# Semaphores from GpSimd to VectorE at the port the two engines share

## The chip, the cores and the metric

The kernel runs on one core of a Trainium2 chip. Five engines of the core take part: TensorE (PE; its weight loads are listed apart as PEld), VectorE (DVE), ScalarE (ACT), GpSimd (POOL) and SyncE (SP), which issues the DMA transfers. The metric is the device time of one execution in microseconds, the median of a few runs.

## The reference

Three layers follow one another, all in float32, for 4 batches of 448 positions:

```python
# 1. causal attention, 12 heads of 64
attn = softmax(mask(q @ k.T / 8)); x = attn @ v          # heads side by side: 768 columns
# 2. gated feed-forward
h = relu(x @ w_in)                                        # 1024 columns
conv = sum(conv_w[k] * shifted(h, k - 1) for k in range(3))
x = (h * sigmoid(conv)) @ w_out
# 3. four experts, each a causal attention with one head of 64, the two best by x @ w_gate
for e in range(4):
    a = softmax(mask((x @ wq[e]) @ (x @ wk[e]).T / 8))
    out += weight_of(e) * (a @ (x @ wv[e]) @ wo[e])
```

## The kernel before

The weights of layer 2's second product and of layer 3's projections are folded into one matrix at the start (`fold`). Operands of the large products are split in a high and a low part, so that each product becomes three matmuls: high by high, low by high, high by low (`products`, L990). For each batch, `ffn_in` makes eight chunks of the gated hidden layer: a ReLU on ACT (L1008), the convolution (L1014 on ACT, two steps of L1019 on DVE), tanh on ACT (L1034), the gate (L1027 on DVE, or L1024 and L1025 on POOL), then the high part (`high`, L696 on ACT, L698 on DVE or L700 on POOL) and the low part (`low`, L704 on DVE or POOL). The last 64 columns of a chunk are copied apart (the tile `gx`, L700 when POOL does it). `project` multiplies the chunks by the folded weights. Attention (`scores`, `norms`, `weigh`) runs on PE (L760 scores, L807 transposes, L838 values), DVE (L737 mask and maximum, L789 division) and ACT (L741 exponential).

Nothing in the code fixes the order of all this by hand. A class `Plan` collects about 4450 steps with their dependencies, their estimated cost on each engine that may do them, and their buffers. `schedule` plays the steps forward in time: each engine takes the ready step of the highest rank. Some steps carry a port (`o.port`): every step that POOL may do counts as using the port when POOL does it, and DVE's steps of the classes copy, scale and subtraction out of SBUF and of the convolution count as using it on DVE. In the plan a step with the port starts only when the port's last user has ended, so that the planned times of such DVE steps and POOL steps do not overlap. `run` then emits all steps in order of planned start. What one engine issues is in that order; what holds between engines on the chip is only what the semaphores say. Besides those of the data there is one kind more: where a POOL step comes within 3 us of planned time behind a DVE step with the port, `run` makes POOL's first instruction wait by semaphore for DVE's last (`near`, `add_manual_dep`). In the other direction, DVE behind POOL, there was none.

Of the kernel before, what the change touches and what calls it, by code (L numbers as in the profile page):

```python
# [182 lines left out]
def noise(seed, n):  # L183

    x = (n * 2654435761 + seed * 40503 + 12345) & 0xFFFFFFFF
    for shift, factor in ((15, 0x2C1B3C6D), (12, 0x297A2D39), (15, 1)):
        x = ((x ^ x >> shift) * factor) & 0xFFFFFFFF
    return x / 2147483648.0 - 1.0
# [43 lines left out]
class Plan:  # L232
# [135 lines left out]
    def run(self):  # L368


        self.links()
        left = [(b, b.left) for t in self.tags.values() for b in t.made]
        kinds = {id(t.kind): (t.kind, dict(t.kind.free)) for t in self.tags.values()}

        def forward(rank):
            for b, n in left:
                b.left, b.ap = n, None
                for k in b.banks or ():
                    k.end, k.engine = 0.0, None
            for t in self.tags.values():  # L380
                t.next = t.live = 0
            for k, tiles in kinds.values():
                k.free = dict(tiles)
            return self.schedule(rank)

        rank = self.longest()
        length = forward(rank)
        best = (length, rank)
        for _ in range(ROUNDS):
            if length == float("inf"):  # L390
                break
            rank = self.backward()
            length = forward(rank)
            best = min(best, (length, rank))
        rank = list(best[1])
        forward(rank)
        begin = [o.start for o in self.ops]
        for seed, lo, hi, amp in SHIFTS:
            for o in self.ops:
                if seed < 0:  # L400
                    rank[o.n] += amp * (lo <= o.n < hi)
                elif lo <= begin[o.n] < hi:
                    rank[o.n] += amp * noise(seed, o.n)
        if SHIFTS and forward(rank) >= best[0]:
            forward(best[1])
        body, near = self.nc.cur_bb.bb, None
        for o in sorted(self.ops, key=lambda o: (o.start, o.n)):
            n = len(body.instructions)
            o.fn(o.engine)
            new = body.instructions[n:]  # L410
            if o.engine == "V" and "V" in o.port:
                near = o, new[-1].name
            elif o.engine == "G" and near and near[0].start > o.start - 3:
                self.tc.add_manual_dep(new[0], near[1], mybir.DependencyInfo(mybir.DependencyClass.Sync, mybir.DependencyReason.DATA), reason="port")

    def schedule(self, rank):
        for o in self.ops:
# [152 lines left out]
class Cost(dict):  # L570


    port = "V"
# [670 lines left out]
```

## Time and profile before

| | us |
|---|---|
| median of 3 runs | 521.71 (521.52 to 522.1) |
| the profiled execution | 521.82 |
| its span | 520.0 |
| PE busy | 510.4 (98%) |
| DVE busy | 416.7 (80%) |
| ACT busy | 357.4 (69%) |
| POOL busy | 79.3 (15%), 86 instructions |

The span is what the profiler saw of the program; the execution's own time is 1.8 us longer. Busy time is a sum over an engine's instructions and says nothing of what an instruction does in its time: one that is held counts as busy. PE's granted clock is at its upper level (2.4 GHz) throughout.

### The profile page before, as it was taken

How to read it: one execution, taken by the hardware profiler on the slowest of the kernel's cores; microseconds unless marked ns; L12 is line 12 of the kernel's file. 1: busy time of each engine (PE TensorE's matmuls, PEld its weight loads, DVE VectorE, ACT ScalarE, POOL GpSimd, SP SyncE). 2: the span in 40 equal slices, each digit the busy share in tenths (PEclk: the TensorE clock that was granted, in tenths of full speed). 3: DMA queues.
4: the chain of work that ended last, by engine and by line, in shares of the span. 5: the costliest groups of instructions: out<-in, count | busy, mean ns of one | idle time of the engine just before them, and what ended most of it. 6: DMA issues, size and time to landing. Idle time of an engine off the chain costs nothing.

```text
span 520.0 us, 10393 instructions
## 1 busy us (share of the span) xinstructions
PE 510.4 (98%) x3556; PEld 434.5 (84%) x3556; DVE 416.7 (80%) x1313; ACT 357.4 (69%) x1062; POOL 79.3 (15%) x86
## 2 busy tenths in 40 slices
PE   8799999999999999999999999999999999999997
PEld 4678888878888988999897878988888878999875
DVE  6999699999999098997478999996359999852681
ACT  2887377789999175863569988984269967532573
POOL 3122011242324000101014320130022001000000
PEclk9999999999999999999999999999999999999999
DMA  8885356674885100649101573663021505610052
GB/s 251 237 225 146 98 166 202 195 201 146 293 249 126 41 20 20 226 144 277 24 2 37 155 222 94 240 184 89 0 55 63 184 2 186 232 68 1 2 168 106
DMA packets 63524, 69.92 MB, mean 134 GB/s; under 512 B 36592, under 2 KB 57456, under 8 KB 63472
## 3 DMA queue, kind: packets, MB, share of 16 engines
q1 hardware_dynamic: 63472, 69.26, 44.6%
q8 instruction: 28, 0.46, 0.4%
q14 instruction: 24, 0.20, 0.1%
HBM read 55.87 MB, written 13.37 MB: 133 GB/s over the span
## 4 chain that ended last, share of the span: by engine, by line
PE 86%; DVE 8%; ACT 3%; DMA 1%; issue 1%; SPq 0%; ACTq 0%
PE pf L990 56%; PE bank L838 9%; PE bank L807 9%; PE bank L760 8%; DVE e L737 3%; PE pf L1187 2%; DVE e L789 2%; DMA work<-in_wqk 1%; ACT e L741 1%; PE pf L1098 1%; DVE z L698 1%; PE bank L990 1%; ACT e L786 1%; DVE pair L704 1%; PE pf L675 1%
## 5 line engine op out<-in xcount | busy, mean ns | idle before, releaser
L990 PE MATMUL pf<-pair,slab 128*128 128x448 f32 (+2 forms) x984 | 216.7, 366 | 0.9 <-ACT pair L696 0.7
L990 PEld LDWEIGHTS pf<-pair,slab 128*128 128x128 f32 x984 | 171.0, 188 | 18.6 <-ACT pair L696 1.2
L741 ACT ACTIVATE e<-e,stat 128x320 f32<-128x320 f32 (+3 forms) x256 | 127.1, 500 | 17.7 <-DVE stat L737 17.4
L737 DVE CUSTOM_DVE_ANT_0 e<-bank,mask 64x64 f32<-64x64 f32 (+3 forms) x256 | 93.1, 413 | 16.4 <-PE bank L760 15.6
L990 PE MATMUL pf<-pair,wqks 128*128 128x448 f32 x384 | 82.2, 370 | 0.0
L990 PEld LDWEIGHTS pf<-pair,wqks 128*128 128x128 f32 x384 | 70.9, 188 | 6.4 <-DVE pair L698 0.3
L807 PE MATMUL bank<-ident,e 128*128 128x128 f32 x448 | 71.0, 276 | 0.9 <-ACT e L741 0.2
L696 ACT ACTIVATE z<-bank 128x512 f32<-128x512 f32 (+1 forms) x133 | 53.2, 421 | 15.2 <-PE bank L838 8.5
L807 PEld LDWEIGHTS bank<-ident,e 128*128 128x128 f32 x448 | 53.7, 140 | 9.6 <-DVE stat L737 0.7
L704 POOL TENSOR_TENSOR pair<-work,pair 128x448 fp32r<-128x448 f32 (+1 forms) x35 | 42.6, 1236 | 87.4 <-DVE work L913 33.6
L786 ACT ACTIVATE e<-e,stat 64x64 f32<-64x64 f32 (+3 forms) x129 | 52.0, 448 | 4.6 <-DVE stat L781 3.6
L698 DVE COPY z<-bank 64x128 f32<-64x128 f32 (+1 forms) x91 | 38.0, 434 | 20.9 <-PE bank L807 11.9
L760 PE MATMUL bank<-pair,pair 64*128 64x448 f32 (+3 forms) x576 | 49.6, 291 | 0.0
L741 ACT ACTIVATION_READ_ACCUMULATOR e<-e,stat 128x1 f32 (+1 forms) x256 | 48.8, 191 | 0.0
L838 PE MATMUL bank<-z,block 128*64 128x448 f32 (+3 forms) x384 | 46.9, 386 | 0.0
L760 PEld LDWEIGHTS bank<-pair,pair 64*128 64x128 f32 (+1 forms) x576 | 42.4, 172 | 2.3 <-issue 0.8
L838 PEld LDWEIGHTS bank<-z,block 128*64 128x64 f32 x384 | 25.8, 136 | 21.0 <-issue 12.0
L1019 DVE SCALAR_TENSOR_TENSOR work<-hp,cws,work 128x448 f32<-128x448 f32 x64 | 42.8, 682 | 0.4
L990 PE MATMUL pf<-wvs,pair 128*128 128x260 f32 x288 | 39.6, 288 | 0.0
L700 POOL TENSOR_SCALAR pair<-work 128x896 fp32r<-128x896 f32 (+2 forms) x17 | 15.2, 895 | 145.4 <-DMA block<-in_vv 43.7
L990 PEld LDWEIGHTS pf<-wvs,pair 128*128 128x128 f32 x288 | 36.2, 189 | 0.5
L696 ACT ACTIVATE pair<-pf 64x448 fp32r<-64x448 f32 (+1 forms) x24 | 13.0, 542 | 32.0 <-PE pf L990 31.2
(98 smaller groups left out, 568.5 us busy)
## 6 DMA issues: line engine op xcount, KB each, us to landing
slab<-w_scratch SPq DMA_DIRECT2D x24, 768.0 KB, 4.6
work<-in_w_out SPq DMA_DIRECT2D x8, 768.0 KB, 4.9
work<-in_w_in SPq DMA_DIRECT2D x8, 768.0 KB, 6.0
w_scratch<-slab SPq DMA_DIRECT2D x8, 768.0 KB, 4.1
work<-in_qk SPq DMA_DIRECT2D x24, 224.0 KB, 4.4
work<-in_qk SPq DMA_DIRECT2D x48, 112.0 KB, 3.9
out<-work SPq DMA_DIRECT2D x23, 224.0 KB, 2.0
slab<-wo_scratch SPq DMA_DIRECT2D x6, 768.0 KB, 4.4
```

Source lines behind the costliest of these rows:

```text
L696: nc.scalar.activation(dst(), src(), AF.Copy)
L698: nc.vector.tensor_copy(dst(), src())
L700: nc.gpsimd.tensor_scalar(dst(), src(), 1.0, 1.0, op0=OP.mult, op1=OP.mult)
L704: return lambda e: engine(e).tensor_sub(dst(), src(), f32(h()))
L737: nc.vector.tensor_tensor_reduce(out=ec(o, c), in0=bank(o, c), in1=m, scale=-0.125, scalar=3.0e38, op0=OP.add, op1=OP.min, accum_out=st[ro ...
L741: nc.scalar.activation(ec(o, c), ec(o, c), AF.Exp, bias=st[rows, 0, o, c:c + 1], scale=-1.0, accum_out=st[rows, 1, o, c:c + 1])
L760: nc.tensor.matmul(bank(o, c), q(s)[own, Q0[c]:Q0[c] + QN[c]], k(t)[own, kc(o, c)], start=i == 0, stop=i == 2)
L786: nc.scalar.activation(dst(), src(), AF.Copy, scale=st[rows, 3, o, c:c + 1])
L807: P.op({"T": TURN}, lambda _: nc.tensor.transpose(dst(), src(), ident[:, :]), r=r, w=keys)
L838: nc.tensor.matmul(ps[own, S - n:S], v(k, o), z[:, 1024 * o + n0:1024 * o + n0 + n], start=k == 0, stop=k == 3)
L990: nc.tensor.matmul(out_ap(), a(), b(), start=first, stop=end), r=r, w=[(ps, 0)])
L1019: return lambda _: nc.vector.scalar_tensor_tensor(cv[:, :S], hp[:, i:S + i], cws[:, fc, i:i + 1], cv[:, :S], op0=OP.mult, op1=OP.add)
```

## The change

`near` becomes a record of the last step with the port on each of the two engines. A POOL step looks for the last DVE step with the port, as before; a DVE step with the port now looks for the last POOL step. If that one's planned start lies less than 3 us back, the new step's first instruction waits by semaphore for the other step's last. The order and the costs are not touched.

```diff
-        body, near = self.nc.cur_bb.bb, None
+        body, near = self.nc.cur_bb.bb, {}
...
-            if o.engine == "V" and "V" in o.port:
-                near = o, new[-1].name
-            elif o.engine == "G" and near and near[0].start > o.start - 3:
-                self.tc.add_manual_dep(new[0], near[1], mybir.DependencyInfo(mybir.DependencyClass.Sync, mybir.DependencyReason.DATA), reason="port")
+            if o.engine == "G" or o.engine == "V" and "V" in o.port:
+                other = near.get("VG"[o.engine == "V"])
+                if other and other[0].start > o.start - 3:
+                    self.tc.add_manual_dep(new[0], other[1], mybir.DependencyInfo(mybir.DependencyClass.Sync, mybir.DependencyReason.DATA), reason="port")
+                near[o.engine] = o, new[-1].name
```

No engine's instructions change their order; what changes are the semaphores that DVE's instructions wait for. A wait that another one implies is left out by the framework, so some rows also lose one. Line numbers after the change are one higher. Two places follow; a name in brackets is the engine whose semaphore a row waits for, and a number behind a tile's name is the buffer.

The first is DVE where the last chunks of batch 0's hidden layer are made, at about 161 to 163 us of the profile, before:

```order
L1027 SCALAR_TENSOR_TENSOR work_150<-work_150,hp_95 128x448 [waits Activation_49]
L698 CAST pair_134<-work_150 128x448 [waits DVE_49]
L704 TENSOR_TENSOR pair_134<-work_150,pair_134 128x448 [waits DVE_49]
L779 TENSOR_REDUCE stat_87<-stat_87 128x8 [waits Activation_49]
L781 RECIPROCAL stat_87<-stat_87 128x8 [waits DVE_49]
L789 TENSOR_SCALAR e_124<-e_124,stat_87 128x320 [waits DVE_49]
```

and after the change:

```order
L1028 SCALAR_TENSOR_TENSOR work_150<-work_150,hp_95 128x448 [waits Activation_49]
L699 CAST pair_134<-work_150 128x448 [waits Pool_49]
L705 TENSOR_TENSOR pair_134<-work_150,pair_134 128x448 [waits Pool_49]
L780 TENSOR_REDUCE stat_87<-stat_87 128x8 [waits Activation_49]
L782 RECIPROCAL stat_87<-stat_87 128x8 [waits DVE_49]
L790 TENSOR_SCALAR e_124<-e_124,stat_87 128x320 [waits DVE_49,Pool_49]
```

The cast (high part), the subtraction (low part) and the first division each wait for POOL now, each for another of the three `gx` copies, which POOL issues in a row and which waited for DVE already.

The second is DVE in the hidden layer of batch 2, at about 329 to 333 us, before:

```order
L698 COPY z_114<-bank_155 128x4x128 [waits PE_49]
L1019 SCALAR_TENSOR_TENSOR work_150<-hp_96,cws,work_150 128x448 [waits Activation_49]
L1027 SCALAR_TENSOR_TENSOR work_150<-work_150,hp_95 128x448 [waits Activation_49]
L1019 SCALAR_TENSOR_TENSOR work_150<-hp_96,cws,work_150 128x448 [waits DVE_49]
L779 TENSOR_REDUCE stat_87<-stat_87 128x8 [waits Activation_49]
L781 RECIPROCAL stat_87<-stat_87 128x8 [waits DVE_49]
L789 TENSOR_SCALAR e_124<-e_124,stat_87 128x320 [waits DVE_49]
```

and after the change:

```order
L699 COPY z_114<-bank_155 128x4x128 [waits PE_49]
L1020 SCALAR_TENSOR_TENSOR work_150<-hp_96,cws,work_150 128x448 [waits Activation_49,Pool_49]
L1028 SCALAR_TENSOR_TENSOR work_150<-work_150,hp_95 128x448 [waits Activation_49]
L1020 SCALAR_TENSOR_TENSOR work_150<-hp_96,cws,work_150 128x448 [waits DVE_49]
L780 TENSOR_REDUCE stat_87<-stat_87 128x8 [waits Activation_49]
L782 RECIPROCAL stat_87<-stat_87 128x8 [waits DVE_49]
L790 TENSOR_SCALAR e_124<-e_124,stat_87 128x320 [waits DVE_49,Pool_49]
```

One convolution step and one division got a wait for POOL, which at this time makes high parts of layer 1's operands for a later head pair and of this layer's chunks.

## Rows read from the trace of the kernel before

**Rows 1.** The page, part 1: busy time, share of the span, instructions.
```profile
PE 510.4 (98%) x3556; PEld 434.5 (84%) x3556; DVE 416.7 (80%) x1313; ACT 357.4 (69%) x1062; POOL 79.3 (15%) x86
```

**Rows 2.** Busy time by stretch: stretch, length, PE, PEld, DVE, ACT, POOL, clock, DMA, GB/s.
```profile
94.80:167.80 73.00, 72.87 (x503) 60.06 (x503) 72.05 (x214) 68.94 (x205) 24.94 (x25) 1.00 0.68 205
322.50:352.30 29.80, 29.80 (x172) 26.54 (x169) 29.43 (x89) 27.62 (x80) 5.74 (x7) 1.00 0.69 229
...
32.00:520.00 488.00, 483.78 (x3398) 417.06 (x3397) 390.40 (x1218) 337.17 (x1014) 69.97 (x73) 1.00 0.42 127
```

**Rows 3.** DVE's waits in 94.8:167.8, then 322.5:352.3: us in total, times, longest.
```profile
DVE e L737 <- PE bank L760: 0.3, 1, 0.3
...
DVE e L737 <- ACT work L1014: 0.5, 1, 0.5
```

**Rows 4.** Timeline of POOL and DVE near 98 and 129: start, us, what.
```profile
96.60 1.84 POOL L704 TENSOR_TENSOR slab<-work,slab 128x768 fp32r<-128x768 f32 x1
...
97.81 1.10 DVE L698 CAST pair<-work 128x896 fp32r<-128x896 f32 x1
...
127.84 1.85 POOL L704 TENSOR_TENSOR slab<-work,slab 128x768 fp32r<-128x768 f32 x1
...
129.39 0.79 DVE L1019 SCALAR_TENSOR_TENSOR work<-hp,cws,work 128x448 f32<-128x448 f32 x1
...
130.10 0.67 DVE L1019 SCALAR_TENSOR_TENSOR work<-hp,cws,work 128x448 f32<-128x448 f32 x1
```

**Rows 5.** Timeline of POOL and ACT near 438; in brackets the idle time before.
```profile
437.62 0.98 POOL L1025 TENSOR_TENSOR work<-work,hp 128x448 f32<-128x448 f32 x1
...
438.63 0.58 ACT L696 ACTIVATE pair<-work 128x448 fp32r<-128x448 f32 x1 [1.12 <-POOL work L1025]
```

**Rows 6.** Timeline of DVE and POOL near 162.
```profile
161.71 0.39 DVE L698 CAST pair<-work 128x448 fp32r<-128x448 f32 x1
...
161.77 0.49 POOL L700 TENSOR_SCALAR gx<-pair 128x128 fp32r<-128x128 f32 x1 [4.21 <-DVE work L1027]
...
162.14 0.62 DVE L704 TENSOR_TENSOR pair<-work,pair 128x448 fp32r<-128x448 f32 x1
...
162.26 0.66 POOL L700 TENSOR_SCALAR gx<-pair 128x128 fp32r<-128x128 f32 x1
...
162.90 0.30 POOL L700 TENSOR_SCALAR gx<-pair 128x128 fp32r<-128x128 f32 x1
```

**Rows 7.** Timeline of PE's weight loads (and one DVE cast); in brackets idle time before.
```profile
153.62 0.14 PEld L807 LDWEIGHTS bank<-ident,e 128*128 128x128 f32 x1 [0.21 <-DVE stat L737]
...
163.23 0.19 PEld L990 LDWEIGHTS pf<-pair,wqks 128*128 128x128 f32 x1
...
351.90 0.39 DVE L698 CAST pair<-work 128x448 fp32r<-128x448 f32 x1
...
352.35 0.19 PEld L990 LDWEIGHTS pf<-pair,wqks 128*128 128x128 f32 x1 [0.34 <-DVE pair L698]
```

**Rows 8.** Timeline of POOL and DVE in the second stretch.
```profile
329.43 0.94 POOL L700 TENSOR_SCALAR pair<-work 128x896 fp32r<-128x896 f32 x1 [17.75 <-DVE stat L737]
...
329.94 0.89 DVE L1019 SCALAR_TENSOR_TENSOR work<-hp,cws,work 128x448 f32<-128x448 f32 x1
...
349.41 0.96 POOL L700 TENSOR_SCALAR pair<-work 128x896 fp32r<-128x896 f32 x1 [1.78 <-DVE stat L779]
...
350.21 0.31 DVE L789 TENSOR_SCALAR e<-e,stat 128x192 f32<-128x192 f32 x1
```

**Rows 9.** Timeline of DVE and PE's weight loads near 239.
```profile
238.38 0.39 DVE L698 CAST pair<-work 128x448 fp32r<-128x448 f32 x1
...
239.86 0.19 PEld L990 LDWEIGHTS pf<-pair,wqks 128*128 128x128 f32 x1
```

**Rows 10.** Waits of PE's weight loads, 160 to 320: us in total, times, longest.
```profile
PEld bank L807 <- DVE stat L737: 0.5, 1, 0.5
PEld bank L807 <- ACT e L741: 0.4, 1, 0.4
```

## The prediction

> **What bounds the kernel now.** I read the busy times of the page first: TensorE (PE) is busy for 510.4 us of a span of 520.0, VectorE (DVE) for 416.7 [rows 1]. An average of 80% would say that DVE has room, so I looked at stretches. From 94.8 to 167.8 us DVE is busy for 72.05 of 73.00 us while PE is busy for 72.87, and from 322.5 to 352.3 for 29.43 of 29.80 [rows 2]. In each of them DVE waits for another engine once, for 0.3 and 0.5 us, both at its beginning [rows 3]. There DVE is a second bound: what is added to one of its instructions reaches all that follow, until DVE next waits for somebody. So the question is not how much DVE time is added in all, but how much in these stretches, and which PE instruction reads DVE's last result just in time.
>
> **What GpSimd and DVE do to each other before.** The change concerns places where the plan puts a GpSimd (POOL) step shortly ahead of a DVE step that needs the port. Two kinds of row show what happens there without a semaphore.
>
> In the first kind DVE comes second and is held inside its instruction. A subtraction on POOL starts at 127.84 and takes 1.85, so it ends at 129.69. DVE's L1019 starts at 129.39, takes 0.79 instead of the 0.67 that the same instruction takes right after it, and ends at 130.18, 0.49 after POOL's end [rows 4]. So it is held, but not for its whole length: about 0.18 of it is over when POOL ends. The copy at 97.81 is the same case: it ends at 98.91, 0.47 after POOL's 98.44 [rows 4].
>
> In the second kind DVE comes first, by a few hundredths, and POOL is held. At 161.71 DVE starts a cast (0.39), at 161.77 POOL starts a gx copy that takes 0.49; the next pair, 162.14 and 162.26, is alike, POOL taking 0.66. The third copy, at 162.90, meets no DVE instruction of this kind in its beginning and takes 0.30 [rows 6].
>
> **The change part by part.** No instruction is added, removed or moved on PE, ACT, SP or POOL; DVE's rows keep their order too, and 37 of them wait for POOL where 21 did. DVE waits in its order, so every DVE instruction behind such a wait stands with it. 34 POOL steps are now awaited by a first DVE step. I laid their ends beside the starts of those DVE instructions: for 14 POOL had ended before, and such a wait costs nothing. That leaves 20.
>
> *Price of a hand-off.* The trace has no tight wait of DVE for POOL. The nearest rows are ACT's wait for POOL, 437.62 + 0.98 = 438.60 to 438.63, so 0.03 [rows 5], and from below nothing (POOL long done); from above POOL's own wait for DVE: the cast ends at 162.10, POOL starts at 162.26, so 0.16 [rows 6]. I take 0.03, as the waiting engine is the one that reacts and POOL is the slow one to start. Then the first kind costs 0.03 + 0.67 - 0.49 = 0.21 for an L1019, and 0.15 to 0.25 for the other forms: DVE's instruction now begins after POOL has ended, where before it had begun and stood ready.
>
> The Trainium skill, page "SBUF — State Buffer", section "Who interferes with whom", says that the pair of ports is an exclusive lock, and that whichever comes second is blocked until the first is finished. By it the DVE instruction would have run its full length after POOL's end already, and a wait would add the hand-off alone. The rows agree that there is a lock and that POOL is held too, but not that the whole length comes after. What it would make of the time is the first rival below.
>
> *Stretch 1, until 153.6.* Overlaps of the first kind at 97.81, 129.39 and 142.78 (the first two in [rows 4], the third read alike) add 0.18 + 0.21 + 0.16 = 0.55 to DVE. At 153.62 PE's weight load waits for DVE (0.21 of idle time behind it) [rows 7]: no slack, so PE is 0.55 later.
>
> *Stretch 1, the three gx copies.* At 157.4 there is one more of the first kind, 0.21. Then the plan's order is DVE cast, POOL gx, DVE low part, POOL gx, each now strictly in turn. The first gx goes 161.77 to 162.07 (0.30 alone), the cast 162.10 to 162.49: +0.39. POOL takes 0.16 to start and 0.30: 162.65 to 162.95; the low part then starts at 162.98 instead of 162.14: +0.84, of which 0.39 was counted. DVE is by then 0.55 + 0.21 + 0.84 = 1.60 late. PE loads the weights of the product that reads this low part at 163.23 [rows 7]; it ended at 162.76, and a weight load follows DVE's end by 0.06 (351.90 + 0.39 to 352.35) [rows 7], so the slack is 0.41. PE is 1.60 - 0.41 = 1.19 late, so 0.64 more. The third gx copy adds 0.13 to DVE alone, which stops being busy throughout a few us later and sheds its own lateness; PE does not.
>
> *215 to 240 us.* Four overlaps, two of each kind, add about 2 x 0.2 + 2 x 0.4 = 1.2 to DVE. The cast at 238.38 ends at 238.77 and PE's weight load that reads it is at 239.86 [rows 9]: slack 1.03 after the 0.06. I count 0.1.
>
> *Stretch 2.* Three overlaps of the first kind: at 329.94 (0.89 instead of 0.67, ending 0.46 after POOL) +0.24, the next like it +0.24, the last at 350.21 (0.31, ending at 350.52, 0.15 after POOL's 350.37) +0.20, and 0.02 at 347.65, where POOL ended just before [rows 8]; 0.70 in all. The weight load at 352.35 stood 0.34 for DVE [rows 7]: no slack, 0.70 to PE.
>
> *Elsewhere.* The other five overlaps (47.8, 70.5, 193.9, 438.5 and 448.5) lie outside the two stretches, where DVE waits for other engines within some microseconds; I count none. If that cover were gone they would cost about 0.2 each.
>
> **Sum:** 0.55 + 0.64 + 0.10 + 0.70 = 1.99 us. Between the two stretches PE's weight loads wait once for 0.5 us for DVE and once for 0.4 for ACT [rows 10], in the softmax. These chains start from PE's own scores, so most of the lateness passes through them, but a late PE may wait less there: I take off 0.2, a little under a quarter of the 0.9, and keep 1.8. The profiled execution took 521.82 with its span of 520.0, 0.11 above the median of 521.71. The span becomes 521.8, the median 523.5.
>
> **The rivals.**
>
> 1. *The lock already costs the whole length*, so a wait adds 0.03. Then 0.09 reaches PE by 153.6; 0.03 + 0.84 more on DVE by 163.2, less 0.41, makes 0.55; stretch 2 adds 0.12. That is +0.7, 522.4, which is not slower by 0.2%. Against it are the 0.49 and 0.47 after POOL's end; for it, that ends on POOL may be recorded late. It decides if the same rows after the change again end 0.5, and not 0.7, behind POOL. The rule of the page "SBUF — State Buffer" of the Trainium skill gives this rival.
> 2. *A hand-off costs 0.16, as POOL's wait for DVE does.* 0.13 more for each wait that counts: three by 153.6, three by 163.2, four between 215 and 240, four in stretch 2: 14 x 0.13 = 1.8 on top, 525.3.
> 3. *Nothing arrives.* The order of work is the same, and the 0.95 us in which DVE is not busy in stretch 1 (73.00 - 72.05) [rows 2], which I take for fixed starting costs, might be slack. Then 0.95 + 0.41 there and 0.37 in stretch 2 take up nearly all: 521.7 to 522.0.
> 4. *Faster:* gx copies on POOL end sooner, 0.49 and 0.66 becoming 0.30. All that PE is not busy after 32 us is 488.00 - 483.78 = 4.2 us [rows 2]. A gain must come out of these, and POOL's earlier ends would have to be what PE waited for there; with 0.3 for it 521.4.
>
> That the change does nothing is excluded by the added waits of which 20 meet a running POOL.
>
> **How the numbers follow.** A measurement of this kernel can tell about 0.2%, 1.04 us, from no change: below 520.67 is faster, above 522.75 slower. Forecast, 522.75 to 524.4 (upward 14 x 0.04 for a hand-off of 0.07 and the 0.3 by which the runs differ; downward what is absorbed of the terms): 0.66. Rival 1: 0.15. Rival 2: 0.10. Rival 3: 0.05. Rival 4: 0.04. Slower is 0.66 + 0.10 = 0.76, same 0.15 + 0.05 = 0.20, and rival 4 stands as 0.04 for faster, since a gain that I overlooked would be of its kind. The range takes in the forecast and rival 1 and leaves out 0.19: 522.3 to 524.4.
>
> **What would show it.** In the profile after, the L1019 at about 129.4 should start 0.03 after POOL's end and take 0.67, not 0.79; the low part after the cast near 162 should start some 0.8 later relative to the cast; the gx copies should take 0.30. PE's total of busy time should stay, and its span grow at the weight loads that now wait longer for DVE near 153.6, 163.2 and 352.4, about 0.6 each; before 94 us both traces should agree to a tenth. I am wrong if L1019 again ends 0.5 after POOL, or if PE shows no longer wait for DVE at these three places.

## The result and the profile after

| | before | after |
|---|---|---|
| median, first set (4 runs each) | 521.62 (521.15 to 522.1) | 524.28 (523.95 to 524.48) |
| ratio to before, 95% interval | | 1.0054 (1.004 to 1.0068) |
| the profiled execution | 521.82 | 524.33 |
| its span | 520.0 | 522.5 |
| two more sets later, medians | 521.16, 521.61 | 522.96, 523.17 |
| their ratios | | 1.0034 (1.002 to 1.0047), 1.003 (1.002 to 1.004) |

The change makes the kernel slower, by 2.7 us in the first set and by 1.8 and 1.6 us in the later ones (e11 and e12 below). The forecast was +1.8 us, 523.5 in a range of 522.3 to 524.4. The first set lies at the upper end of that range: its median just inside, and 521.71 times its ratio, 524.5, just outside. A ratio is the one on record with its interval; it is close to the quotient of the two medians, but not the same (524.28 by 521.62 is 1.0051). So there are two questions: are the terms of the sum right, and what made the first set larger?

The page's line of busy time after the change answers to [rows 1]:

```profile
PE 511.1 (98%) x3556; PEld 433.6 (83%) x3556; DVE 415.5 (80%) x1313; ACT 357.2 (68%) x1062; POOL 77.7 (15%) x86
```

No engine has more to do. DVE and POOL are even busy for less, 415.5 for 416.7 and 77.7 for 79.3 us: time in which an instruction was held and counted as busy now stands as idle time between instructions. Busy time would call this a gain, and the kernel is slower.

The timeline of POOL and DVE after the change (start, us, what, in brackets the idle time before and what ended it), at the places of [rows 4, 6, 8]:

```profile
96.40 1.83 POOL L705 TENSOR_TENSOR slab<-work,slab 128x768 fp32r<-128x768 f32 x1
...
98.26 0.63 DVE L699 CAST pair<-work 128x896 fp32r<-128x896 f32 x1 [0.56 <-POOL slab L705]
...
126.29 3.63 POOL L705 TENSOR_TENSOR slab<-work,slab 128x768 fp32r<-128x768 f32 x2 [9.35 <-DVE stat L780]
...
129.96 0.69 DVE L1020 SCALAR_TENSOR_TENSOR work<-hp,cws,work 128x448 f32<-128x448 f32 x1 [0.22 <-POOL slab L705]
...
162.63 0.30 POOL L701 TENSOR_SCALAR gx<-pair 128x128 fp32r<-128x128 f32 x1 [4.43 <-DVE work L1028]
162.97 0.39 DVE L699 CAST pair<-work 128x448 fp32r<-128x448 f32 x1 [0.42 <-POOL gx L701]
163.51 0.30 POOL L701 TENSOR_SCALAR gx<-pair 128x128 fp32r<-128x128 f32 x1 [0.58 <-DVE pair L699]
163.85 0.62 DVE L705 TENSOR_TENSOR pair<-work,pair 128x448 fp32r<-128x448 f32 x1 [0.49 <-POOL gx L701]
...
331.22 0.94 POOL L701 TENSOR_SCALAR pair<-work 128x896 fp32r<-128x896 f32 x1 [17.76 <-DVE stat L738]
...
332.20 0.69 DVE L1020 SCALAR_TENSOR_TENSOR work<-hp,cws,work 128x448 f32<-128x448 f32 x1 [0.38 <-POOL pair L701]
```

Each DVE instruction that waits starts 0.03 to 0.04 us behind POOL's end (98.23 to 98.26, 129.92 to 129.96, 162.93 to 162.97, 163.81 to 163.85, 332.16 to 332.20) and then takes its whole length: 0.63 in place of 1.10, 0.69 for 0.79, 0.69 for 0.89. It ends 0.66 to 0.73 behind POOL, where it ended 0.46 to 0.49 behind it before. That is the price of a hand-off of the first kind, some 0.2 us. The gx copies take 0.30 each, and POOL follows DVE's cast after 0.15 (163.36 to 163.51). Here the order on the chip is turned round as well: before, the cast started 0.06 ahead of the first copy [rows 6], and now it waits for that copy.

PE's weight loads at the places of [rows 7]:

```profile
154.28 0.14 PEld L808 LDWEIGHTS bank<-ident,e 128*128 128x128 f32 x1 [0.65 <-DVE stat L738]
164.53 0.30 PEld L991 LDWEIGHTS pf<-pair,wqks 128*128 128x128 f32 x2 [0.41 <-DVE pair L705]
354.83 1.32 PEld L991 LDWEIGHTS pf<-pair,wqks 128*128 128x128 f32 x7 [1.01 <-DVE pair L699]
```

All three wait longer for DVE: 0.65 for 0.21, 0.41 for nothing, 1.01 for 0.34. They grew by 0.44, 0.41 and 0.67.

To see where the lateness arises I matched each weight load of a trace with the same one of the trace before, and took how much later it starts; a stretch costs what this lateness grows by between its ends (worked out from the traces; the places are times of before, each the median over the 3 us behind it). The first row is the lateness at 100 us. It arises in the first 34 us, before any added wait has moved the matmuls, and says nothing of the change: in two executions of programs without the added waits, e8 and e6 below, it is -0.79 and -1.47. The last row is the length of one small DVE instruction near 298, which is explained under the table; it took 0.61 before the change.

| | after | e11 | e12 | e10 | e2 | e3 | e4 | e5 | e1 |
|---|---|---|---|---|---|---|---|---|---|
| at 100 | -0.19 | -1.03 | -0.69 | -1.12 | -1.09 | -0.99 | 0.00 | -0.21 | -0.79 |
| 100 to 118 | +0.46 | +0.19 | +0.19 | +1.43 | +0.18 | +0.01 | +0.17 | +1.07 | +0.64 |
| 118 to 154 | +0.41 | +0.65 | +0.39 | +0.36 | +0.40 | -0.08 | -0.08 | -0.09 | -0.01 |
| 154 to 167 | +0.63 | +0.67 | +0.67 | +0.68 | +0.62 | +0.09 | +0.42 | -0.01 | +0.11 |
| 167 to 245 | +0.09 | +0.08 | +0.03 | +0.06 | -0.07 | 0.00 | +0.02 | +0.03 | 0.00 |
| 245 to 293 | +0.02 | +0.07 | 0.00 | +0.12 | -0.13 | -0.03 | -0.01 | +0.14 | +0.01 |
| 293 to 303 | +0.39 | -0.25 | +0.42 | -0.43 | +0.20 | +0.06 | -0.09 | -0.43 | +0.13 |
| 303 to 353 | +0.67 | +0.75 | +0.66 | +0.66 | +0.02 | +0.69 | -0.02 | -0.01 | +0.03 |
| 353 to 512 | +0.01 | +0.01 | +0.01 | -0.12 | -0.14 | +0.02 | +0.02 | +0.04 | -0.02 |
| length near 298, us | 1.01 | 0.35 | 1.01 | 0.12 | 0.80 | 0.66 | 0.50 | 0.13 | 0.72 |

"After", e11 and e12 are the same program in three executions. They agree to 0.1 us at 154 to 167, 167 to 245 and 303 to 353. They differ at 100 to 118, at 118 to 154 (e11 alone) and most of all at 293 to 303, by 0.67. In the first trace two things there went against the change. At 110 DVE's L910 waits for a transfer that had landed in time before. It is the first of three integer instructions that turn a loaded weight's 64-bit words into float32; the expectations below call it the hash, and so does this text from here on:

```profile
110.36 0.56 DVE L910 TENSOR_SCALAR work<-work 128x768 int32<-128x768 int32 x1 [0.18 <-DMA work<-in_w_in]
```

And near 298 a small instruction was held by POOL. It belongs to the gate of layer 3, which weighs the experts (not to layer 2's gate, L1027), is the first of that gate behind its exponential, and carries no wait, since the plan doesn't mark it with the port. Before (start, us, what):

```profile
297.72 1.16 POOL L704 TENSOR_TENSOR pair<-work,pair 128x448 fp32r<-128x448 f32 x1
...
298.30 0.61 DVE L1139 TENSOR_TENSOR work<-work 128x16 f32<-128x16 f32 x1
```

and after:

```profile
297.39 0.94 POOL L701 TENSOR_SCALAR pair<-work 128x896 fp32r<-128x896 f32 x1 [9.14 <-DMA work<-in_qk]
298.42 2.27 POOL L705 TENSOR_TENSOR pair<-work,pair 128x448 fp32r<-128x448 f32 x2
...
299.71 1.01 DVE L1140 TENSOR_TENSOR work<-work 128x16 f32<-128x16 f32 x1
```

It is tiny (16 columns; 0.12 us where nothing holds it, e8 and e10) and ends 0.03 to 0.04 behind POOL's second subtraction in both. POOL began when its input landed: 4.8 us after the issue in the trace after, 4.4 before. So DVE was 1.41 late when it came there and 1.81 when it left.

The matmuls follow this instruction. In all nine columns of the table the step at 293 to 303 is its length less 0.61, to within 0.07: +0.40 and +0.39, -0.26 and -0.25, and so on. It holds in the other four traces as well: e6 0.38 and -0.23, e7 0.68 and +0.08, e8 0.12 and -0.42, e13 0.13 and -0.42.

### The profile page after: what moved, and what is told of

Same layout as the page of the kernel before. It is cut to its first block, busy times and chain, and to the rows that moved or that the text cites. A ratio compares the mean times of both kernels' runs of the same rounds, so it can differ in the third digit from the quotient of the medians.

```text
span 522.5 us, 10404 instructions
## 1 busy us (share of the span) xinstructions
PE 511.1 (98%) x3556; PEld 433.6 (83%) x3556; DVE 415.5 (80%) x1313; ACT 357.2 (68%) x1062; POOL 77.7 (15%) x86
## 5 line engine op out<-in xcount | busy, mean ns | idle before, releaser
L1020 DVE SCALAR_TENSOR_TENSOR work<-hp,cws,work 128x448 f32<-128x448 f32 x64 | 42.6, 679 | 1.4 <-POOL pair L701 0.4
L790 DVE TENSOR_SCALAR e<-e,stat 64x64 f32<-64x64 f32 (+3 forms) x111 | 32.2, 329 | 2.5 <-POOL pair L705 0.5
```

The source lines that it names most:

```text
L790: engine(en).tensor_scalar(dst(), src(), st[rows, 3, o, c:c + 1], gate, op0=OP.mult, op1=OP.mult)
L1020: return lambda _: nc.vector.scalar_tensor_tensor(cv[:, :S], hp[:, i:S + i], cws[:, fc, i:i + 1], cv[:, :S], op0=OP.mult, op1=OP.add)
```

## The experiments

Theory A: the time is paid where DVE stands until POOL's instruction ends, at the places and prices of the prediction; what lies beside that is the landing of transfers.

### e1: the same waits on a POOL step that has long ended

```diff
-                if other and other[0].start > o.start - 3:
-                    self.tc.add_manual_dep(new[0], other[1], mybir.DependencyInfo(mybir.DependencyClass.Sync, mybir.DependencyReason.DATA), reason="port")
-                near[o.engine] = o, new[-1].name
+                last = near.get("old") if o.engine == "V" else other
+                if other and last and other[0].start > o.start - 3:
+                    self.tc.add_manual_dep(new[0], last[1], mybir.DependencyInfo(mybir.DependencyClass.Sync, mybir.DependencyReason.DATA), reason="port")
+                near["old" if o.engine == "G" else "-"], near[o.engine] = near.get(o.engine), (o, new[-1].name)
```

> VectorE's marked instructions still carry a semaphore wait on GpSimd, but on the GpSimd step before the last, which has long ended: 43 waits on VectorE, all true on arrival at the first and second stretch. Theory A (each us is paid because VectorE stands still until a GpSimd instruction that is still running ends): the +2.5 us are gone, 521.6 to 521.9 us, and at 153.6, 163 and 352 us the matmuls stand where they stood before to within 0.15 us. Rival B (the semaphores, their increments on GpSimd and the added instructions cost it, wherever they stand): 523 to 524.3 us, as the changed kernel.

521.78 us against 521.47, ratio 1.0007 (0.9998 to 1.0017). The cast at 98 is held inside its instruction again, as before, in spite of its wait:

```profile
95.80 1.83 POOL L706 TENSOR_TENSOR slab<-work,slab 128x768 fp32r<-128x768 f32 x1
...
97.02 1.10 DVE L700 CAST pair<-work 128x896 fp32r<-128x896 f32 x1
```

In the table 118 to 154, 154 to 167 and 303 to 353 are within 0.11 of nothing. The 0.64 between 100 and 118 is the hash's transfer, which the profile names with 0.54 us of idle time. So neither the semaphores nor the added instructions cost anything that the trace shows, and the interval leaves room for 0.9 us at most, where the changed kernel lost 1.6 to 2.7; rival B falls.

### e2, e3, e4: the waits of one place alone

```diff
-                if other and other[0].start > o.start - 3:
+                if other and other[0].start > o.start - 3 and (o.engine == "G" or 94 < o.start < 168):
```

That is e2; e3 has `322 < o.start < 356` and e4 `161.5 < o.start < 164`.

> The changed kernel with VectorE's waits only on instructions planned between 94 and 168 us, 24 in all. Theory A (the cost stands where the waits stand): the matmuls are 0.65 us late at 153.6, 1.1 to 1.3 us late by 166, and nothing is added at 352: 522.8 us. Theory A2 (as A, but a shift ahead of the softmax stretch also makes GpSimd's cast near 296 us, which a transfer releases, later than the shift, so that GpSimd's two subtractions hold the gate's first small VectorE instruction longer): another 0.4 us at 302, the small instruction takes 1.0 us in place of 0.61, 523.3 us. Rival B (the cost is spread over all waits): 24 of 43 waits, 523.0 us, with no step at 153.6 or 163.

522.66 against 521.47, 1.0023 (1.0012 to 1.0033). The matmuls lose 0.18, 0.40 and 0.62 in the three parts of the first stretch, 1.2 us by 167, and 0.02 at 353. At 293 to 303 another 0.20 were lost, half of A2's 0.4, with 0.13 and 0.14 given back ahead of it and behind it; the gate's small instruction took 0.80 us. Rival B, with no step at 153.6 or 163, falls.

> The changed kernel with VectorE's waits only on instructions planned between 322 and 356 us, 23 in all. Theory A: nothing before 322, the matmuls 0.67 us late from 352.4 on: 522.3 us. Theory A2: the same, and the gate's small instruction near 298 us takes its 0.61 us as before, since nothing is shifted ahead of it. Rival B (spread over all waits): 523.0 us. Rival C (an earlier delay is what makes the one at 352 appear): 521.6 to 521.8 us.

522.14 against the same runs, 1.0018 (1.0006 to 1.0029). Nothing over 0.1 in any row before 303, then 0.69. The place looks as in the changed kernel; it comes 2.7 us earlier, as no wait ahead has delayed it and the opening was 0.8 us quicker:

```profile
328.48 0.94 POOL L701 TENSOR_SCALAR pair<-work 128x896 fp32r<-128x896 f32 x1 [17.77 <-DVE stat L738]
...
329.46 0.69 DVE L1020 SCALAR_TENSOR_TENSOR work<-hp,cws,work 128x448 f32<-128x448 f32 x1 [0.38 <-POOL pair L701]
```

Rival C falls: no earlier delay is needed.

> The changed kernel with VectorE's waits only on the three copies planned near 162 us, 22 waits in all. By the prediction's own step: VectorE 0.84 us late behind the three copies, less 0.41 us of slack that the delays ahead had used up in the changed kernel: matmuls +0.43 us at 163, 522.1 us. Rival 1 (no slack): +0.64 to +0.84 us, 522.4 us. Rival 2 (the port already kept the two apart there, so the order is free): 521.6 to 521.8 us.

521.74 in the median, 1.0013 (1.0003 to 1.0023). By the medians that is 0.3 us and by the ratio 0.7; the noise of the sets is as large, and the trace decides. In the table +0.42 at 154 to 167, where the prediction's step said 0.84 - 0.41 = 0.43. Both the price and the slack were read rightly from [rows 6, 7], and rivals 1 and 2 of this run fall.

### e5: the waits everywhere else

```diff
-                if other and other[0].start > o.start - 3:
+                if other and other[0].start > o.start - 3 and (o.engine == "G" or not (94 < o.start < 168 or 322 < o.start < 356)):
```

> The changed kernel with VectorE's waits everywhere but on instructions planned between 94 and 168 and between 322 and 356 us, 31 in all. By the prediction's sum: 0.1 us near 240 us, nothing elsewhere: 521.3 us beside 521.2, and no difference that can be told from none. Rival (the softmax stretch and the rest carry what the two stretches don't, 0.5 to 0.8 us): 521.7 to 522.0 us, with steps of the matmuls outside the two stretches.

521.75 against 521.61, 1.0002 (0.9991 to 1.0013). At 215 to 240 the matmuls lose 0.03, though DVE is for a while 1.15 us later than it was at 215, as in the changed kernel: it sheds this again by 242. Outside the two stretches the waits cost the matmuls nothing that this trace shows, and the rival falls. What moved in this trace is two transfers, in both directions. The hash at 110 waited a whole microsecond,

```profile
110.96 0.56 DVE L910 TENSOR_SCALAR work<-work 128x768 int32<-128x768 int32 x1 [0.97 <-DMA work<-in_w_in]
```

and the gate's instruction was hardly held, 0.13 us, which gives back 0.43 at 303.

### e11, e12: the changed kernel again, unchanged

> The changed kernel once more, unchanged, for a second trace and more times on the chip and against the same runs of the kernel before as the next three. In its first trace the matmuls lost 0.27 us at 110 (VectorE's hash waited for a transfer) and 0.41 us at 298 (GpSimd's cast waited for a transfer that took 4.78 us; 4.25 to 4.49 us in the traces of e1 to e4), which the waits don't explain. Theory A (these two are chance of the transfers): in this trace at least one of them is gone, and the steps of the waits alone, 0.17 at 98, 0.40 at 154, 0.55 to 0.65 to 167, 0.1 at 240 and 0.67 at 352, come back to within 0.1 us each; median 523.4 to 523.9 us. Theory B (the later cast follows from the waits): the transfer takes over 4.7 us again, the gate's small instruction 0.9 to 1.0 us, and the median is 524.0 to 524.5 us.

522.96 against 521.16, 1.0034 (1.002 to 1.0047): lower than expected, +1.8. The hash waits for nothing here, and the gate (the second of POOL's subtractions, then DVE):

```profile
298.09 1.15 POOL L705 TENSOR_TENSOR pair<-work,pair 128x448 fp32r<-128x448 f32 x1
...
298.93 0.35 DVE L1140 TENSOR_TENSOR work<-work 128x16 f32<-128x16 f32 x1
```

The transfer ahead took 4.2 us from issue to landing. The small instruction is 0.26 shorter than before the change, and the matmuls gain 0.25. So the +0.4 at 302 doesn't come with the waits each time, and theory B, by which it does, falls. One step missed the expectation: 0.65 at 118 to 154, not 0.40. Some 0.2 of it is a DVE cast that stood 0.33 us at 116.2; in the first trace and in e12 it stood 0.07 and 0.06, and I can't say why.

> The changed kernel a third time, unchanged. Its first four runs stood 2.7 us above the kernel before, the second set of seven 1.8 us. Theory A (the waits cost 1.9 to 2.0 us, and what lies above or below is the landing of transfers, which differs from execution to execution): 1.6 to 2.2 us above; in its trace the gate's small instruction near 298 ends 0.03 us behind GpSimd's second subtraction wherever it is held, and the matmuls at 302 move by as much as that instruction's length differs from 0.61 us. Theory B (the first set shows the cost, 2.7 us, and the second was luck): 2.4 us or more above.

523.17 against 521.61, 1.003 (1.002 to 1.004): +1.6. In its trace the gate's instruction is held as long as in the first one:

```profile
298.71 1.15 POOL L705 TENSOR_TENSOR pair<-work,pair 128x448 fp32r<-128x448 f32 x1
...
298.88 1.01 DVE L1140 TENSOR_TENSOR work<-work 128x16 f32<-128x16 f32 x1
```

with 4.8 us from issue to landing and +0.42 at 303. So an execution with the long hold may stand in a set with +1.6: the hold differs from execution to execution. The signs of theory A hold, and its theory B, 2.4 us or more, falls. Two of the three executions of the changed kernel have the long hold, and no trace of another kernel has one over 0.80; whether the waits make it likelier, three executions can't tell.

### e10, e8, e6: the transfer that the gate depends on

The transfer that POOL's cast near 296 waits for is issued ahead of two output transfers, in the changed kernel (e10) and in the one before (e8):

```diff
         body, near = self.nc.cur_bb.bb, {}
+        self.ops[3266].start = self.ops[2798].start - 0.01
         for o in sorted(self.ops, key=lambda o: (o.start, o.n)):
```

> The changed kernel with one transfer, the one that GpSimd's cast near 296 us waits for, issued one place ahead of two output transfers on SyncE's queue, so about 1.1 us earlier. Theory A (the gate's first small VectorE instruction, which carries no wait, is held by GpSimd's two subtractions until they end): GpSimd ends about 1 us earlier, the small instruction falls from 1.0 us to 0.2 to 0.3 us, and the matmuls at 302 lose nothing in place of 0.4 us: 0.3 to 0.8 us less than the changed kernel, about 523.5 us where that gives 524.2. Rival (the matmuls at 302 were late for another reason): no difference from the changed kernel.

> The kernel before with the same transfer issued one place ahead of two output transfers. Theory A: the gate's small instruction falls from 0.61 to about 0.2 us, since GpSimd's subtractions end ahead of it, VectorE is up to 0.4 us early at 299, and the matmuls up to 0.3 us early at 302: 521.3 to 521.5 us. Rival (TensorE has other work there, so that VectorE's 0.4 us is hidden): no difference from the kernel before.

In both traces the gate's instruction is free. e10:

```profile
298.47 1.15 POOL L706 TENSOR_TENSOR pair<-work,pair 128x448 fp32r<-128x448 f32 x1
...
299.83 0.12 DVE L1141 TENSOR_TENSOR work<-work 128x16 f32<-128x16 f32 x1
```

and e8:

```profile
294.85 1.14 POOL L705 TENSOR_TENSOR pair<-work,pair 128x448 fp32r<-128x448 f32 x1
...
297.65 0.12 DVE L1140 TENSOR_TENSOR work<-work 128x16 f32<-128x16 f32 x1
```

The matmuls gain 0.43 and 0.42 at 303. This also tells what one of the two waits of [rows 10] was. In the trace before it stands at 301.85,

```profile
301.85 0.14 PEld L807 LDWEIGHTS bank<-ident,e 128*128 128x128 f32 x1 [0.44 <-ACT e L741]
```

and in e8 and e10 no weight load waits for ACT there. Where the hold is long it is joined by a second one, in e12:

```profile
302.14 0.20 PEld L808 LDWEIGHTS bank<-ident,e 128*128 128x128 f32 x2 [0.32 <-ACT e L787]
...
302.83 0.14 PEld L808 LDWEIGHTS bank<-ident,e 128*128 128x128 f32 x1 [0.49 <-ACT e L742]
```

ACT waited for DVE, DVE was held by POOL, and POOL had waited for a transfer. The times don't follow: e10 gives 523.22, 1.0036 (1.0021 to 1.005), no less than e11's 522.96, and e8 521.49 against 521.16, 1.0002 (0.9992 to 1.0012). Runs of one kernel within a set spread by 1.8 to 2.8 us here, much more than the 0.4 us that is looked for. e10's profiled execution lost 1.1 us to the hash's transfer besides, which is most of its +1.43 ahead of 118. So the hold is shown in the traces, and that its removal makes the kernel faster is not shown.

e6 is the kernel before with a small transfer into an unused tile ahead of that one:

```diff
+            if o.n == 3266:
+                self.more()
             o.fn(o.engine)
...
+    spare = base.tile([128, 4], F32, name="spare")
+    P.more = lambda: nc.sync.dma_start(spare[:, :], qk[0, :, 0, :4])
```

> The kernel before with one more small transfer (2 KB, 128 rows of 16 bytes, into a tile that nothing reads) issued just ahead of the one that GpSimd's cast near 296 us waits for. Theory A: the cast and the two subtractions end 0.4 to 0.7 us later, the gate's small instruction grows from 0.61 to 1.0 to 1.3 us, ending 0.03 us behind GpSimd, and the matmuls at 302 are 0.3 to 0.6 us late: 521.9 to 522.2 us. Rival (a later end of GpSimd there is hidden): the small instruction grows and the matmuls at 302 stand as before.

A miss: 520.8 against 521.16, 0.9995 (0.9985 to 1.0005). POOL's cast came 0.22 us earlier against the work around it, the small instruction took 0.38 and the matmuls gained 0.23 at 303, as its length says. The transfer was issued 0.65 later against that work, as meant, but took 3.5 us to land, where it took 4.4 before; the issue alone doesn't fix the landing. The small instruction ends 0.03 to 0.04 behind POOL here as well, as it does in every trace in which it is held. This trace also has a step that nothing here explains: +0.45 at 167 to 245, with no wait added. So a single step of that size, seen once, shows nothing by itself; the steps above are believed because they recur.

### e7, e13: without POOL's waits too

```diff
-                if other and other[0].start > o.start - 3:
+                if False:
```

> No waits of this kind on either engine: GpSimd's, which the kernel before has, are taken out too (21 waits left, of data). Theory A (where two instructions meet at the port, the second is held inside its own instruction until the first ends, and that costs no more than a semaphore, less by some 0.17 us where the held one's own work overlaps): the same as the kernel before or up to 0.5 us faster, 520.7 to 521.3 us. Rival (an instruction that starts beside another at the port slows both, so that GpSimd's waits are worth their price): 0.5 us slower or more.

> As the one without such waits on either engine, and the transfer for GpSimd's cast near 296 us issued ahead of two output transfers, as in e8. If both help as their theories say: 520.4 to 520.9 us, 0.3 us or more under the kernel before, with the gate's small instruction at 0.12 us. If neither moves the end: 521.2 us.

530.67 against 521.61, 1.0174 (1.0159 to 1.019), and 530.06, 1.0164 (1.0148 to 1.0179): both about 9 us slower. The expectation had the wrong sign. The page of e7:

```profile
PE 513.9 (97%) x3556; PEld 434.7 (82%) x3556; DVE 425.8 (80%) x1313; ACT 357.4 (67%) x1062; POOL 85.9 (16%) x86
```

DVE is busy for 9.1 us more than before and POOL for 6.6 more, with the same instructions: each is held by the other. Two places, POOL and DVE in the order of time:

```profile
119.58 2.10 POOL L705 TENSOR_TENSOR slab<-work,slab 128x768 fp32r<-128x768 f32 x1 [2.04 <-DVE slab L699]
119.89 2.27 DVE L1020 SCALAR_TENSOR_TENSOR work<-hp,cws,work 128x448 f32<-128x448 f32 x1
...
162.92 0.94 POOL L701 TENSOR_SCALAR pair<-work 128x896 fp32r<-128x896 f32 x1
163.01 1.06 DVE L790 TENSOR_SCALAR e<-e,stat 128x384 f32<-128x384 f32 x1
163.94 1.16 POOL L705 TENSOR_TENSOR pair<-work,pair 128x448 fp32r<-128x448 f32 x1
163.99 1.58 DVE L705 TENSOR_TENSOR pair<-work,pair 128x448 fp32r<-128x448 f32 x1
165.50 1.54 DVE L1028 SCALAR_TENSOR_TENSOR work<-work,hp 128x448 f32<-128x448 f32 x1
```

At 119.58 POOL begins a subtraction that ran at 126.06 before, since its data are ready, and DVE's L1020, 0.31 us behind it, takes 2.27 in place of 0.67. It ends 0.48 behind POOL, as in [rows 4]. Near 163 POOL works through a cast and subtractions that the plan had put after DVE's, and three DVE instructions take 1.06, 1.58 and 1.54 in place of 0.42, 0.62 and 0.62, while POOL takes its usual 0.94 and 1.16. So one is held until the other is done; that both are slowed, as the rival had it, is not what the rows show. From 118 to 167 the matmuls lose 5.9 us in e7 and 4.3 in e13, and 2.21 and 2.35 in the second stretch. About 1.1 us of e7's 5.9 is not the port: PE's granted clock stood at its lower level (1.2 GHz) from 167.8 to 171.2 us of that trace, after PE had waited 2.19 us for DVE. In e13 PE waited 2.31 us there and kept the upper level, and it is almost as slow as e7 in the end, so the clock doesn't carry the 9 us. At these places nothing but its waits for DVE had kept POOL from taking the port ahead of the plan. In e13 the gate's instruction is free (0.13) and the matmuls gain 0.42 at 303, as in e8 and e10.

## Why the prediction was right in its terms and where it failed

**The bound.** Right. In the two stretches what DVE lost arrived at PE, less the slack that was read for the gx copies (table), and between them DVE could be 1.15 us later without PE (e5).

**The hand-off** was priced at 0.03 from ACT's wait for POOL [rows 5] and is 0.03 to 0.04. The other end, 0.16 from [rows 6], is what POOL needs after DVE, 0.15 again. Rival 2 falls. The overlaps at 97.81, 129.39, 142.78 and 157.4 cost DVE 0.16, 0.20, 0.19 and 0.21 in the first trace, where the prediction had 0.18, 0.21, 0.16 and 0.21.

**Rival 1**, that the lock costs the whole length anyway, falls with the rows at 129.96 and 332.20. The Trainium skill, page "SBUF — State Buffer", section "Who interferes with whom", has the second instruction fully blocked until the first is finished. It is blocked; but it ends 0.46 to 0.49 behind POOL where it takes 0.63 to 0.69 alone, so about 0.2 of its length doesn't follow POOL's end, and a wait by semaphore gives just this away. Here the rows decide. Whether DVE does that part while it is held, as the prediction says, or POOL gives the port up some 0.2 before its recorded end, no run here tells; the price is the same.

**The terms.** By 154: 0.55 predicted; 0.19 + 0.39 = 0.58 in e12, and 0.87 in the first trace with 0.27 of it the hash's transfer. The three gx copies: 0.64; 0.63 to 0.68. 215 to 240: 0.10; 0.03 to 0.09. The second stretch: 0.70; 0.66 to 0.75. Their sum was put at 1.99; in the first trace they make (0.46 - 0.27) + 0.41 + 0.63 + 0.09 + 0.67 = 1.99, in e12 1.94, in e10 without the transfer (DVE lost 1.23 to it) 1.96. In e11 they make 2.34, of which 0.26 is what 118 to 154 took above e12. At 215 to 240 the prediction's own figures, 1.2 less 1.03, give 0.17 and not the 0.1 that it counted; DVE did lose 1.15 there, and 0.03 to 0.09 arrived.

**The signs.** The L1019, the gx copies and the three longer waits of PE came as forecast, if with 0.44, 0.41 and 0.67 for "about 0.6 each". Two signs did not. The low part near 162 starts 0.45 later relative to its cast, not 0.8; the 0.84 holds only with the cast's own 0.39, as the prediction's working has it. And "before 94 us both traces should agree to a tenth" is wrong: the openings differ by 0.19 in the first trace and by up to 1.1 in the others, whatever the kernel.

**The step that failed** is the last one before the forecast: "a late PE may wait less there: I take off 0.2". Nothing was taken off. The wait of 0.5 for DVE in [rows 10] stayed at 0.52 to 0.55 in the three traces of the changed kernel. The wait of 0.4 for ACT was not slack of the softmax but the gate's instruction held by POOL, and POOL's beginning hangs on a transfer. Its size in the matmuls was +0.39, -0.25 and +0.42 in three executions of the changed kernel. I had read who ended that wait and not followed it back: ACT, DVE, POOL, DMA. The place should have been a term of about -0.4 to +0.4 in the range and of nothing in the sum. The range had no such term: above the forecast it allowed 0.56 for a dearer hand-off and "the 0.3 by which the runs differ", read from three runs, while 35 later runs of the kernel before spread from 520.09 to 522.79.

**The size of the first set.** Its profiled execution lost 1.99 + 0.39 (gate) + 0.27 (hash) = 2.65 us of the 2.68 that it lost behind 100 us; its opening gave 0.19 back, so that it stood 2.51 above the profiled execution of before. So nearly all of what this execution lost is accounted for. That such transfers differ between executions is shown (0 to 1.1 us of waiting at 110, and 0.18 of it also in e13, which has none of the added waits; 0.13 to 1.01 us for the gate's instruction with the queue as it was). Why all four runs of that set lay within 0.5 us of each other, while e11's seven spread over 2.3, stays open: only one of the four has a trace, and a difference between chips isn't excluded, as the later sets ran on two others than e1 to e4 and the first set's chip isn't on record. The intervals of the ratios are 2.1 to 3.5 us for this set and 1.0 to 2.5 and 1.0 to 2.1 for the two later ones; 1.99 lies in both of the later ones and just below the first. That the later sets, +1.8 and +1.6, agree with the forecast's number is luck: the traces give no 0.2 to take off, and what lies between 1.99 and these medians is within what transfers and openings move.

**Rivals 3 and 4** fall with the interval, which is above 1 in all three sets, and rival 3 with the table too: the steps arrive at PE. "That the change does nothing" falls with the rows.

## What to carry to other kernels

Where two engines share a lock, a semaphore that only repeats the order in which they take it anyway costs a hand-off and loses the overlap: here 0.2 us for each, in stretches where the waiting engine has no slack, and about 0.4 where it makes two engines take turns that had run side by side. The semaphores that keep the slow engine from taking the lock early were worth about 9 us in the same kernel (e7). So look at which wait changes the order for the better, and put waits only there. And follow a wait in a stretch "with slack" back to its first cause before counting on it; where that is a transfer, it belongs in the range. Read the spread of the runs from more than three of them.

## What the runs showed of the hardware

- DVE's instruction that comes second at the port ends 0.46 to 0.49 us behind POOL (casts of 128x896 and L1019), though it takes 0.63 to 0.69 alone: about 0.2 us of it doesn't come after POOL's recorded end. Started by a semaphore, it ends 0.66 to 0.73 behind.
- A semaphore from POOL reaches DVE 0.03 to 0.04 us after the recorded end, and one from DVE reaches POOL after 0.15 to 0.16. Semaphores that are true on arrival cost nothing that e1's trace shows; its ratio is 1.0007 (0.9998 to 1.0017).
- A DVE instruction of 16 columns with both inputs in the on-chip memory, 0.12 us alone, took up to 1.01 us behind a POOL subtraction (first trace and e12). The section of the Trainium skill named above counts a DVE instruction with two such inputs among those that contend with a POOL instruction that reads that memory, and names no size; the rows agree. The plan here left this one unmarked.
- Issue to landing of one 224 KB transfer took 4.2, 4.4, 4.8 and 4.8 us in four executions in which the queue held the same transfers (e11, before, after, e12).
- PE's granted clock fell to its lower level at 167.8 us of e7, after PE had waited 2.19 us for DVE, and stayed at the upper one in e13 after a wait of 2.31 us.
